# Two more blocks of transposed x by DMA transposes, with the order tables written anew, in a kernel of chunk-selected attention and a gated MLP

## The chip, the cores and the metric

The kernel runs on one core of a Trainium2 chip. The time is device microseconds of one execution (the core's span and what lies around it). Times of a kernel are given as the median of several runs; the trace is of one more execution, which has a time of its own.

## What is computed

For each of 4 batches and 8 heads, 768 queries of 64 elements attend to keys that are taken in chunks of 32. Each query picks six chunks by an upper bound on its scores, and attends causally within them. The heads, side by side, are x; a gated MLP with a mixing over the sequence follows:

```python
k_min = np.min(k_chunks, axis=3)          # k in chunks of 32
k_max = np.max(k_chunks, axis=3)
ub = sum(max(q * k_min, q * k_max))       # one bound per query and chunk
ub = np.where(causal, ub, -1e9)
top_chunks = np.argsort(ub)[..., -6:]
scores = q @ k.T / sqrt(64)               # masked: chosen chunks, causal
x = softmax(scores) @ v                   # heads side by side: 4 x 768 x 512
h = gelu(x @ w_in)                        # tanh form; 512 -> 1024
u, v = h[..., :512], h[..., 512:]
v_n = (v - mean(v)) / sqrt(var(v) + 1e-6) * g_ln
v_s = w_sg @ v_n + b_sg                   # over the 768 positions
out = x + (u * v_s) @ w_out
```

## The kernel before

The work goes by pairs of heads, 16 of them (p, or r where the scores of an earlier pair are meant), four pairs to a batch. A pair has these steps.

- *Loads* (`load_rows`, L541; `load_v`, L552): rows of k, q and v come in as kn, qn and vn, 128 rows to a partition block, all issued by SyncE (SP). Three buffers of each go round.
- *Transposes of k and q* (`kside` L635, `qside` L679, through `rows_T` L559): TensorE (PE) transposes 128×128 blocks in f32 into PSUM (tile PSG, L562). VectorE (DVE) reduces k to a minimum and a maximum for each chunk (W, L657), and ACT or DVE copies k and q out (KA, qT; the copies have the lines of the helper `copier`, L301 on ACT, L302 on DVE and GpSimd (POOL)). POOL or ACT casts qT to QA, and rT is the positive part of qT (L690 or L693). For the last four pairs k is transposed by DMA (L590) instead, and its extremes by DVE.
- *Selection* (`select` L708, `select_full` L761): PE forms the bounds (L730, L777), DVE transposes them (U), finds the eight largest (L747, L797), compares (Dn) and transposes back (Dt, L757, L805). From pair 4 on, rows of Dt are copied into QA by DMA (L810), so that one matmul adds the mask; for the first four pairs PE adds it with IND by matmuls of its own (L893).
- *Scores and softmax* (`scores` L862, `scores_full` L826): PE multiplies into PSC (L887, L847), ACT takes the exponential into E (L902, L853), POOL clears what lies above the diagonal (L909, L858).
- *Values* (`head` L913): PE multiplies E by vx, which holds v and a column of ones (L925, L932); DVE takes the reciprocal of the sum (L940) and writes the scaled rows to XS (L942).
- *Transposed x* (`xtrans` L947): one block of 128 columns of x, that is one pair, is transposed into xT. Either PE does six 128×128 transposes in bf16 into PSUM (L959) and DVE or ACT copies the block out, or one DMA transpose issued by SP does it all (L951). The tuple XDMA (L327) names the blocks (batch, dk) that go by DMA: before, all four of batch 2 and three of batch 3.

When the four blocks of a batch are there, `moe_h` and `moe_g` (L965, L1027) run the MLP: PE multiplies xT by w_in (L974 for the half that is normalized, L1018 for the other); ACT takes the Gelu (L979, L1023), which needs another function table than the exponential; DVE takes means and variances (L987, L989); POOL the root (L1004); DVE the normalization (vhat, L1007). PE mixes over the sequence (L1035), DVE scales, adds the bias and multiplies by u (L1053, L1057), PE multiplies by w_out (L1069), DVE adds x (L1086), and SP stores (L1091). xT, uT, vhat and XS are kept twice, for two batches; in the early part parts of them are staging places for w_in, w_out and w_sg.

The batches overlap: while batch b is in the MLP, the pairs of batch b+1 are in attention. What sets the order is not the order of the code. The code makes a list of operations, each with what it reads and writes (1309 of them). The constant TABLE at the end has, for each engine, the list of operation numbers in the order in which the engine runs them; the PSUM bank of each tile ("slots"); the engine of each operation that may run on several ("choice", one letter each); and a few filler matmuls at the start. `place` and `link` (L101, L123) add the waits that this order needs: an engine runs its list in order, and waits by semaphore for what it reads, for a bank to come free, and for a buffer. All DMAs of the kernel are in SP's list, so one whose data is not there yet holds those behind it.

Of the kernel before, what the change touches and what calls it, by code (L numbers as in the profile page):

```python
# [261 lines left out]
def _build(nc, ctx, q, k, v, w_in, g_ln, w_sg, b_sg, w_out, out):  # L262
# [64 lines left out]
    XDMA = tuple((2, d) for d in range(NDK)) + tuple((3, d) for d in range(3))  # L327
# [213 lines left out]
    def load_rows(p, nm, src, dst):  # L541
        s = p % NQS
        for h0, h1 in ((0, 1), (1, 2)) if p < SPLIT else ((0, 2),):
            for i in range(2):
                j0, j1 = 3 * h0, 3 * h1
                P.op("act" if i == 1 and p < BOTH else "sp", lambda e, i=i, j0=j0, j1=j1: e.dma_start(
                    dst[s][:, j0:j1, i, :], bass.AP(src.tensor, (2 * p + i) * S * DH + 128 * DH * j0,
                                                    [[DH, 128], [128 * DH, j1 - j0], [1, DH]])), dmac(),
                     (nm, p, i, h0), writes=[(nm, s, h, i) for h in range(h0, h1)], dma=f"{nm}{s}_{i}{h0}",
                     xfer=XROW * (h1 - h0) / 2, bulk=NBULK)  # L550
# [8 lines left out]
    def rows_T(src, t, hf):  # L559
        def tr(e):  # L560
            for j in range(3):
                r = e.matmul(t.ap()[:, 128 * j:128 * j + 128],  # L562
                             src[:, 3 * hf + j].rearrange("p i d -> p (i d)"), identF[:], is_transpose=True)
            return r
        return tr
# [69 lines left out]
    def kside(p):  # L635
# [4 lines left out]
        for h0, h1, t in [(hf, hf + 1, ps_g.tile((0, 1, 2, 3))) for hf in range(2)]:  # L640
            ts = [t]

            def tr(e, h0=h0, ts=ts):
                for x, t in enumerate(ts):
                    r = rows_T(kn[s], t, h0 + x)(e)
# [33 lines left out]
    def qside(p):  # L679
        s, w, r = p % NQS, p % NW, p % NR  # L680
        for hf in range(2):
            t = ps_g.tile((0, 1, 2, 3))
            P.op("pe", rows_T(qn[s], t, hf), pe32(*[128] * 3), ("qtr", p, hf), reads=[("qn", s, hf, 0), ("qn", s, hf, 1), "identF"],
# [445 lines left out]
    small_loads()  # L1129
    prep(2)  # L1130
# [9 lines left out]
    for p in range(4, NP + 4):  # L1140
# [4 lines left out]
        if r < NW and HALF < NP:  # L1145
# [31 lines left out]
    "act": (  # L1177
# [9 lines left out]
    "dve": (  # L1187
# [16 lines left out]
    "pool": (  # L1204
# [82 lines left out]
```

## Time and profile before

| what | value |
|---|---|
| median of 3 runs | 208.07 us (207.67 to 208.27) |
| the profiled execution's own time | 208.08 us |
| its span, first to last instruction | 206.0 us |
| PE busy | 197.5 us |
| DVE busy | 186.0 us |
| ACT busy | 162.1 us |
| POOL busy | 92.6 us |
| HBM read and written | 24.87 MB and 6.39 MB |

The span is cut by the first and the last instruction of the program; 2.1 us lie outside it. Busy times are of instructions, and they count an instruction that waits inside its pipeline as busy. PE and the loading of its weights (PEld) overlap. In the rows that follow, "x6" is a count of instructions, a time in us from the start of the span comes first in the timeline and in the chain of waits, and in brackets stands how long the engine was idle before the instruction and what ended that. SPq is the queue of SP. An issue is the instruction that starts a DMA; its data lands later.

### The profile page before, as it was taken

Reading aid. Unit: us, or ns where it says so; the run is one execution under the profiler, and the core shown is the slowest. Engines: PE = TensorE matmul, PEld = TensorE weight load, DVE = VectorE, ACT = ScalarE, POOL = GpSimd, SP = SyncE. Lnnn points to the kernel's source line nnn. Section 1 sums busy time; section 2 is a strip of 40 time slices with the busy share of each in tenths; the row PEclk is TensorE's granted clock in tenths of the full one; section 3 lists DMA queues with packets and bytes.
Section 4 is the critical chain, followed back from the end, with each engine's and each line's share of the span. In section 5 each row is a group of like instructions: output and inputs, shape, how many; then the busy total and the mean of one; then the engine's idle time right before and its main releaser. Section 6 shows DMA issues by size and latency. Waiting matters only on the chain.

```text
span 206.0 us, 5868 instructions
## 1 busy us (share of the span) xinstructions
PE 197.5 (96%) x2294; PEld 131.8 (64%) x2306; DVE 186.0 (90%) x536; ACT 162.1 (79%) x238; POOL 92.6 (45%) x143
## 2 busy tenths in 40 slices
PE   7899999989999999999999999999999999999993
PEld 2547768745775769688456767787456676455551
DVE  4798999989999999999999999998999677897994
ACT  2799999998899988898999889999868986353000
POOL 5254658754665099573534157577221551030000
PEclk9999999999999999999999999999999999999999
DMA  7999999999899769969899947958562445304026
GB/s 150 218 218 219 226 227 307 320 331 234 216 257 235 162 189 234 219 144 189 215 222 221 209 97 194 220 117 86 92 80 41 105 140 112 120 3 151 2 103 253
DMA packets 98378, 36.45 MB, mean 177 GB/s; under 512 B 91952, under 2 KB 93488, under 8 KB 98352
## 3 DMA queue, kind: packets, MB, share of 16 engines
q1 hardware_dynamic: 98352, 36.09, 78.7%
q8 instruction: 18, 0.29, 0.6%
q14 instruction: 8, 0.07, 0.1%
HBM read 24.87 MB, written 6.39 MB: 152 GB/s over the span
## 4 chain that ended last, share of the span: by engine, by line
PE 75%; DVE 10%; ACT 8%; DMA 2%; issue 2%; SPq 1%; DVEq 0%
PE PSG L1035 15%; PE PSC L847 11%; PE PSG L1069 9%; PE PSG L1018 7%; PE PSG L562 7%; PE PSG L925 6%; PE PSG L974 6%; PE PSC L887 3%; ACT E L853 3%; PE PSG L932 2%; PE PSG L777 2%; DMA kn<-in_k_dram 2%; ACT E L902 2%; PE PSC L893 2%; PE PSG L730 2%
## 5 line engine op out<-in xcount | busy, mean ns | idle before, releaser
L853 ACT ACTIVATE E<-PSC 128x1024 bf16<-128x1024 f32 (+1 forms) x72 | 63.2, 915 | 6.7 <-PE PSC L847 5.1
L847 PE MATMUL PSC<-QA,KA 128*128 128x128 bf16 (+2 forms) x336 | 37.7, 246 | 0.2 <-ACT E L853 0.2
L1035 PE MATMUL PSG<-wsgT,vhat 128*128 128x384 bf16 x192 | 34.3, 326 | 0.3 <-DVE vhat L1007 0.3
L858 POOL TENSOR_SCALAR_AFFINE_SELECT E<-E 128x768 bf16<-128x768 bf16 x24 | 20.7, 865 | 24.3 <-ACT E L853 24.3
L847 PEld LDWEIGHTS PSC<-QA,KA 128*128 128x128 bf16 x336 | 24.4, 98 | 8.5 <-ACT E L853 1.5
L657 DVE TENSOR_REDUCE W<-PSG 128x12 f32<-128x384 f32 x48 | 24.2, 546 | 3.2 <-PE PSG L562 3.1
L1035 PEld LDWEIGHTS PSG<-wsgT,vhat 128*128 128x128 bf16 x192 | 18.4, 98 | 11.2 <-DVE vhat L1007 0.5
L1018 PE MATMUL PSG<-xT,winb 128*128 128x384 bf16 x128 | 23.4, 326 | 0.1
L1023 ACT ACTIVATE uT<-PSG 128x384 bf16<-128x384 f32 x32 | 14.5, 492 | 11.2 <-PE PSG L1018 10.8
L1053 DVE SCALAR_TENSOR_TENSOR PSG<-PSG,glnT,bsgbc 128x384 f32<-128x384 f32 x32 | 19.2, 618 | 4.2 <-PE PSG L1035 4.2
L974 PE MATMUL PSG<-winb,xT 128*128 128x512 bf16 x92 | 21.7, 380 | 0.9 <-DVE xT L302 0.6
L1069 PE MATMUL PSG<-woutb,uT 128*128 128x512 bf16 (+1 forms) x92 | 21.6, 370 | 0.4
L302 POOL CAST QA<-qT 64x768 bf16<-64x768 f32 (+1 forms) x19 | 15.6, 821 | 13.9 <-ACT qT L301 13.5
L902 ACT ACTIVATE E<-PSC 128x1024 bf16<-128x1024 f32 (+1 forms) x24 | 20.8, 920 | 0.7 <-PE PSC L893 0.5
L979 ACT ACTIVATE vgb<-PSG 128x512 f32<-128x512 f32 x24 | 14.0, 597 | 7.6 <-PE PSG L974 7.5
L925 PE MATMUL PSG<-vx,E 128*128 128x65 bf16 x480 | 19.4, 194 | 0.1
L925 PEld LDWEIGHTS PSG<-vx,E 128*128 128x128 bf16 x480 | 17.3, 98 | 1.8 <-DVE XS L942 0.3
L942 DVE TENSOR_TENSOR XS<-PSG,rden 128x384 bf16<-128x384 f32 x32 | 17.5, 552 | 0.7
L1018 PEld LDWEIGHTS PSG<-xT,winb 128*128 128x128 bf16 x128 | 12.2, 98 | 8.9 <-ACT uT L1023 0.5
L1057 DVE TENSOR_TENSOR uT<-PSG,uT 128x384 bf16<-128x384 f32 x32 | 17.1, 548 | 0.4
L987 DVE BATCH_NORM_STATS2 stats<-vgb 128x6 f32<-128x512 f32 x24 | 15.9, 683 | 0.8 <-ACT vgb L979 0.7
L974 PEld LDWEIGHTS PSG<-winb,xT 128*128 128x128 bf16 x96 | 8.7, 98 | 11.7 <-ACT vgb L979 2.1
(107 smaller groups left out, 363.9 us busy)
## 6 DMA issues: line engine op xcount, KB each, us to landing
kn<-in_k_dram SPq DMA_DIRECT2D x32, 192.0 KB, 4.4
qn<-in_q_dram SPq DMA_DIRECT2D x32, 192.0 KB, 4.5
vn<-in_v_dram SPq DMA_DIRECT2D x16, 384.0 KB, 4.7
out_dram<-osb SPq DMA_DIRECT2D x18, 256.0 KB, 2.5
uT<-in_moe_w_sg_dram SPq DMA_DIRECT2D x4, 384.0 KB, 5.7
vgb<-in_moe_w_in_dram SPq DMA_DIRECT2D x3, 512.0 KB, 7.8
out_dram<-vgb SPq DMA_DIRECT2D x5, 256.0 KB, 2.1
QA<-Dt SPq DMA_DIRECT2D x24, 36.0 KB, 2.0
```

Source lines behind the costliest of these rows:

```text
L657: P.op("dve", lambda d, m=m, op=op, src=src, h0=h0, h1=h1: d.tensor_reduce(W[w][:, m, 12 * h0:12 * h1].rearrange("p (h c) -> p h c", h=h1 ...
L847: r = e.matmul(t.ap()[:, o:o + n], KA[w][i][:, 128 * kb:128 * kb + 128], QA[w][i][:, q0:q0 + n], start=True, stop=True)
L853: P.op("act", lambda e, t=t, c0=c0, c1=c1, i=i: e.activation(E[es][:, i, c0:c1], t.ap()[:, 0:c1 - c0], ACTF.Exp, scale=SCALE), act(c1 - c0 ...
L858: P.op("pool", lambda g, ev=ev: g.affine_select(ev, ev, pattern=[[0, NT], [1, 128]], compare_op=ALU.is_ge, fill=0.0, base=0, channel_multi ...
L902: P.op("act", lambda e, t=t, c0=c0, c1=c1, n=n: e.activation(E[es][:, :, c0:c1], t.ap().rearrange("p (i x) -> p i x", i=2)[:, :, 0:n], ACT ...
L925: r = e.matmul(t.ap()[:, 65 * qb:65 * qb + 65], E[es][:, i, a:a + 128], vx[w][:, kb, i, :], start=first, stop=False, skip_group_check=True)
L942: P.op("dve", lambda d: d.tensor_tensor(XS[:, b % 2, hh // 2, :, i * DH:(i + 1) * DH], pv3()[:, :, 0:DH], rden[rs][:].rearrange("p (j o) - ...
L974: r = e.matmul(t.ap()[:, 0:F], xT[s][:, dk, 128 * qt:128 * qt + 128], winb[:, dk, F:DFF], start=(dk == 0), stop=(dk == NDK - 1))
L1018: r = e.matmul(t.ap()[:, 0:TG], winb[:, dk, 128 * fb:128 * fb + 128], xT[s][:, dk, TG * tg:TG * tg + TG], start=(dk == 0), stop=(dk == NDK ...
L1035: r = e.matmul(t.ap()[:, 0:TG], vhat[s][:, sb, 128 * fb:128 * fb + 128], wsgT[:, sb, TG * tg:TG * tg + TG], start=(sb == 0), stop=(sb == N ...
L1053: P.op("dve", lambda d, t=t, fb=fb, tg=tg: d.scalar_tensor_tensor(t.ap()[:, 0:TG], t.ap()[:, 0:TG], glnT[:, fb:fb + 1], bsgbc[:, TG * tg:T ...
L1069: r = e.matmul(t.ap()[:, 0:c1 - c0], gT[s][:, fb, 128 * qt:128 * qt + 128], woutb[:, fb, c0:c1], start=(fb == 0), stop=(fb == NF - 1))
```

## The change

Blocks (1, 0) and (1, 1), the first two of the second batch, are put into XDMA. Each loses its six PE transposes and its copy out of PSUM (both copies were DVE's) and becomes one operation of SP. Two PSUM tiles less are taken. The list has 1307 operations, and their numbers after the two blocks move by one and two. In SP's new list the block of pair 5, (1, 1), comes 91st and the block of pair 4, (1, 0), 93rd, with a load of v (pair 10) between them; just ahead of them stand a row of Dt for pair 8 and a load of q (pair 12).

All of TABLE is new: the five orders, the banks and the letters. Besides the two blocks, 58 operations have another engine than before: the lists of DVE, ACT and POOL go from 408, 228 and 139 operations to 404, 225 and 144. At the start ACT's list now begins with two copies of IND (L428), where it began with a copy of CMb (L445); POOL's makes IND's two passes (L424) one right after the other, with one pass of CMb (L440) moved ahead of them; and a cast of QA for pair 1 is on ACT, ahead of its first exponential.

The diff also has a branch that loads rows three to a partition and transposes them so, for the entries of a tuple N3, which is empty; and it moves the call of `mask_rows` for pairs from HALF up to NW to another place, where both of these are 4.

```diff
-    XDMA = tuple((2, d) for d in range(NDK)) + tuple((3, d) for d in range(3))
+    N3 = ()
+    XDMA = tuple((1, d) for d in range(2)) + tuple((2, d) for d in range(NDK)) + tuple((3, d) for d in range(3))
...
     def load_rows(p, nm, src, dst):
         s = p % NQS
+        if (nm, p) in N3:
...
+            return
...
-    def rows_T(src, t, hf):
+    def rows_T(src, t, hf, n3=False):
...
     small_loads()
+    for r in range(HALF, NW):
+        mask_rows(r)
...
-        if r < NW and HALF < NP:
+        if r < HALF and HALF < NP:
             mask_rows(r)
...
 TABLE = {
     "pe": (
-        "1 43 47 52 54 77 81 59 86 88 104 100 186 192 93 190 184 111 109 155 162 194 188 151 160 242 236 116 238 240 198 "
+        "1 43 47 54 52 77 81 59 88 86 100 104 186 192 93 190 184 160 111 109 151 194 188 155 162 242 236 116 202 240 238 "
...
     "sp": (
...
-        "413 347 412 411 553 554 615 298 488 408 409 485 407 551 415 410 350 482 614 612 540 552 613 660 661 663 588 609 "
-        "616 662 608 664 589 611 610 541 506 721 722 697 724 862 555 859 723 649 860 503 861 842 928 509 650 894 863 698 "
+        "413 554 126 552 411 553 346 485 551 488 408 298 407 614 410 482 613 415 409 659 612 611 540 350 661 658 608 660 "
+        "616 615 556 609 722 610 662 607 695 587 859 541 857 720 719 647 721 861 503 588 696 648 840 506 860 509 892 858 "
...
     "filler": (
-        "43:8 54:1 81:2"),
+        "43:8 52:1 81:2"),
```

(In the new list of SP, 616 is block (1, 1), 615 the load of v for pair 10 and 556 block (1, 0).)

More of the change, by code (lines that the diff above doesn't have):

```diff
@@ L542, in load_rows @@
         s = p % NQS
+        if (nm, p) in N3:
+            for h in range(2):
+                P.op("sp", lambda e, h=h: e.dma_start(
+                    dst[s][:].rearrange("p j i d -> p (j i d)")[:, TG * h:TG * h + TG].rearrange("p (i x) -> p i x", i=2),
+                    bass.AP(src.tensor, (2 * p * S + TG * h) * DH, [[3 * DH, 128], [S * DH, 2], [1, 3 * DH]])), dmac(),
+                     (nm, p, h, 3), writes=[(nm, s, h, i) for i in range(2)], dma=f"{nm}{s}_{h}0", xfer=XROW / 2, bulk=NBULK)
+            return
         for h0, h1 in ((0, 1), (1, 2)) if p < SPLIT else ((0, 2),):
@@ L557, in load_v @@
             ("vn", p, 0), writes=[("vn", s)], dma=f"vn{s}", xfer=1880, bulk=NBULK)
-    def rows_T(src, t, hf):
+    def rows_T(src, t, hf, n3=False):
         def tr(e):
             for j in range(3):
+                if n3:
+                    r = e.matmul(t.ap()[:, 0:TG].rearrange("p (x t) -> p t x", t=3)[:, j],
+                                 src[:].rearrange("p j i d -> p (j i d)")[:, TG * hf:TG * hf + TG].rearrange(
+                                     "p (i t d) -> p t i d", i=2, t=3)[:, j], identF[:], is_transpose=True)
+                    continue
                 r = e.matmul(t.ap()[:, 128 * j:128 * j + 128],
@@ L644, in tr @@
                 for x, t in enumerate(ts):
-                    r = rows_T(kn[s], t, h0 + x)(e)
+                    r = rows_T(kn[s], t, h0 + x, ("kn", p) in N3)(e)
                 return r
@@ L682, in qside @@
             t = ps_g.tile((0, 1, 2, 3))
-            P.op("pe", rows_T(qn[s], t, hf), pe32(*[128] * 3), ("qtr", p, hf), reads=[("qn", s, hf, 0), ("qn", s, hf, 1), "identF"],
+            P.op("pe", rows_T(qn[s], t, hf, ("qn", p) in N3), pe32(*[128] * 3), ("qtr", p, hf), reads=[("qn", s, hf, 0), ("qn", s, hf, 1), "identF"],
                  writes=[t], alloc=t)
@@ L1162 @@
     "pe": (
[14 rows of a table removed]
-    "act": (
[9 rows of a table removed]
-    "dve": (
[16 rows of a table removed]
-    "pool": (
[13 rows of a table removed]
[14 rows of a table added]
+    "act": (
[9 rows of a table added]
+    "dve": (
[16 rows of a table added]
+    "pool": (
[14 rows of a table added]
     "slots": (
-        "0132032103013202320333100010001132101220101011331220101110002003230000111233101022200321230101121321323320000311"
-        "1100012112100010122131231201110020033030100110213030322102101203021213233202020013010001111310101121112000010113"
-        "03101011323121013300211302202112100213122010001120010100031100103110011032313330013303100231203011302123"),
+        "3120032313020122323313031310101001202131010113112112000110000301210000111131303023233120231021123123202321030111"
+        "0100132310110001203200231000111220013101100213011201213213110023113212210121013210011033330101100333201011013210"
+        "010100301230210112321013031132122110122101110001010011201100100310011003303230113310020213001323100032"),
     "choice": (
-        "aapdadappapdaadaapppadpddppppdpdpdpdpapadadaapdpappadpdpaadapaappapddpdpdaaapadppapdapapaaaapaapappdapapaaaadaap"
-        "pppddddddddapaappppdadpaapppaddapaappppaaapaappppdddddddppaapaappappppaappppppaappdppaddpdaddpdpddddddddddddd"),
+        "aadadpapappaaapaapapddpaappppdpdpapapaaadapdapppppppdpddadadpadppppddpapaaddpadppppddpapaaaapaappppdapapdaaadadp"
+        "pppdddddddadpaappppaapadpappaapaappppdaapaapappaddddddppaappppppppppaapaapapaapddpdapdppadpdppddddddddddddd"),
     "filler": (
-        "43:8 54:1 81:2"),
+        "43:8 52:1 81:2"),
 }
```

97 rows, old and new, of the table TABLE are left out of this document.

## The prediction

> **What bounds the kernel now.** I read the page first, then the busy time by stage, then the chain of waits, and last the rows around the place of the change. The page:
>
> ```profile
> span 206.0 us, 5868 instructions
> ...
> PE 197.5 (96%) x2294; PEld 131.8 (64%) x2306; DVE 186.0 (90%) x536; ACT 162.1 (79%) x238; POOL 92.6 (45%) x143
> ```
>
> TensorE (PE) is the fullest engine, with VectorE (DVE) close behind. An average over the whole run says little, so here are the stretches around the place of the change, and one late stretch for comparison:
>
> ```profile
> 88.00:92.00 4.00, 4.00 (x77) 3.75 (x74) 4.00 (x10) 3.97 (x6) 3.35 (x4) 1.00 0.57 127
> 92.00:96.00 4.00, 3.89 (x75) 3.42 (x73) 3.90 (x11) 3.44 (x6) 1.98 (x3) 1.00 1.13 237
> 96.00:100.00 4.00, 3.79 (x22) 1.92 (x21) 4.00 (x7) 3.94 (x7) 0.67 (x2) 1.00 0.57 143
> 152.00:156.00 4.00, 4.00 (x42) 2.64 (x41) 4.00 (x28) 3.02 (x8) 0.86 (x1) 1.00 0.51 98
> ```
>
> The columns are the stretch, its length, the busy time of PE, PEld, DVE, ACT and POOL, the granted clock, the share of the DMA engines, and GB/s. From 88 to 92 us PE and DVE are both full and ACT nearly so. No engine is the bound by itself: work taken from one of them alone leaves the others where they are. The clock is granted in full. The chain of waits, in order of time (start, duration, what), shows which engine carries the end of the kernel at the places that matter here:
>
> ```profile
> 12.53 0.85 ACT IND L428
> ...
> 14.06 1.94 ACT E L902 x2
> ...
> 85.39 0.69 DVE osb L1086
> ...
> 88.71 0.47 DVE xT L302
> ...
> 89.87 0.44 DVE xT L302
> ...
> 94.69 0.67 PE PSG L959 x12
> ...
> 97.53 1.28 ACT L979
> 98.83 0.61 ACT vgb L979
> 99.48 2.76 PE PSG L974 x12
> ```
>
> At 12 to 16 us the chain is on ACT. At 85 to 92 us it is on DVE, and the two copies of xT that the change removes (88.71 and 89.87) are pieces of it. At 94.69 it is on PE, in the twelve transposes of the other two blocks. At 97.5 to 99.5 us it is on ACT again: the load of the Gelu table, the first Gelu, and then the matmul that waits for its bank. So the change takes work from two engines that are full and in the chain, and it ends just ahead of a place where a third is.
>
> **The change part by part.** (1) PE loses twelve transposes. What six cost while PE is fed is read from the chain: x12 took 0.67 us at 94.69, and those twelve are the same work for the other two blocks of this batch. So PE loses 0.67 us.
>
> (2) DVE loses the two evacuations, 0.47 + 0.44 = 0.91 us by the chain, or 2 × 542 = 1.08 us by the first row of the group rows below. These sit in the same stage as the PE work. As both engines are full there, the stage shortens by what the less relieved one loses: 0.67 us, and not the sum of both.
>
> (3) SyncE (SP) gets two DMA transposes, and xT waits for their landing. The trace has seven of these already, for the later batches (duration of the issue and then time to landing, min/median/max), and eight of another tile:
>
> ```profile
> L951 SPq DMA_TRANSPOSE xT<-XS x7: 1210/1289/1924, 130.8 to 173.4; - x7
> ...
> DMA to landing us min/median/max: 2.7/2.8/4.3
> ```
>
> ```profile
> L590 SPq DMA_TRANSPOSE KA<-wsb x4: 1225/1296/2398, 127.8 to 164.3; - x4
> ...
> DMA to landing us min/median/max: 2.7/2.9/6.1
> ```
>
> Is that hidden? These are the rows for when the data is there, and for when it is needed:
>
> ```profile
> 87.51 0.54 DVE L942 TENSOR_TENSOR XS<-PSG,rden 128x384 bf16<-128x384 f32 x1
> ...
> 88.63 0.55 DVE L302 COPY xT<-PSG 128x768 bf16<-128x768 bf16 x1
> ...
> 89.10 0.77 DVE L805 STREAM_TRANSPOSE Dt<-Dn 128x576 bf16<-128x576 bf16 x1
> ...
> 89.90 0.55 SPq L810 DMA_DIRECT2D QA<-Dt  x1
> ...
> 90.49 0.58 SPq L554 DMA_DIRECT2D vn<-in_v_dram  x1
> ...
> 91.11 0.71 SPq L546 DMA_DIRECT2D qn<-in_q_dram  x1
> ```
>
> ```profile
> 96.46 2.37 PEld L974 LDWEIGHTS PSG<-winb,xT 128*128 128x128 bf16 x12
> ...
> 99.48 0.55 PEld L974 LDWEIGHTS PSG<-winb,xT 128*128 128x128 bf16 x4 [0.65 <-ACT vgb L979]
> ```
>
> The last block of XS that they need is complete at 87.51 + 0.54 = 88.05. In the new SP order the block of pair 5 goes out behind a row of Dt and a load of q, and the block of pair 4 behind that and a load of v. Dt ends at 89.87 now; in the new DVE order one xT copy (0.55) and the osb addition (0.69) no longer stand ahead of it, so it ends near 88.6. Then 0.55 (row of Dt), 0.71 (q), 1.29 (first transpose) and 0.58 (v) put the second transpose's issue at 91.8. With the median of 2.8 us it lands at 94.6. The first matmul that reads it begins at 96.46 now and 0.67 earlier after the change, at 95.8. The transfer is hidden with 1.2 us to spare, and I cost it at nothing; what hides it is the scores, transposes of q and k and the other two blocks on PE between 91.8 and 95.8. With the longest landings of the rows, 4.3 and 6.1, it would come at 96.1 and 97.9, which is 0.3 and 2.1 us too late. PE already waits 0.65 us at 99.48 for the Gelu, and that much lateness costs nothing. So the bounds of this cost are 0 and 2.1 − 0.65 = 1.45 us; a gain is excluded, since the transfer delivers xT later than PE and DVE did. I take 0, by the row of the same tile. On SP the two issues add 2 × 1.29 = 2.6 us, ahead of the other rows of Dt for pairs 8 and 9 and loads for pairs 11 to 14. Their readers, the scores of pair 9 and the first half of pair 8 and the transposes of later pairs, stand behind the value matmuls of batch 1 in the new PE order, which alone take longer than 2.6 us (2.76 for twelve in the chain, of 24), so nothing queued there is due within the delay.
>
> The Trainium skill, "VectorE: DVE Perf Modes", section "Rules for kernel authors", speaks against this part: it wants a 128×128 transpose on TensorE when PSUM will do, and DMA only otherwise. Its section "The three transpose paths" gives 1309 ns by DMA against 390 ns by TensorE for one such block. By an estimate from that page six blocks one after another are 7.9 us, the landing would be at 99.7, and the sum would rise by 99.7 − 95.8 − 0.65 = 3.2 us. The trace disagrees: whole transposes of six blocks land in 2.7 to 4.3 us there.
>
> (4) All five orders, the banks and the engines of 58 operations are new. Only one part of this can be priced by itself, the start. ACT's first instruction and POOL's mask passes now:
>
> ```profile
> 5.72 0.44 ACT L445 ACTIVATE CMb<-CMb 64x288 bf16<-64x288 bf16 x1 [3.64 <-POOL CMb L440]
> ...
> 8.22 0.84 ACT L301 ACTIVATE QA<-qT 128x768 bf16<-128x768 f32 x1
> ```
>
> ```profile
> 2.99 0.81 POOL L424 TENSOR_SCALAR_AFFINE_SELECT IND<-IND 32x768 bf16<-32x768 bf16 x1 [0.57 <-DVE IND L407]
> ...
> 4.24 0.81 POOL L424 TENSOR_SCALAR_AFFINE_SELECT IND<-IND 32x768 bf16<-32x768 bf16 x1
> ```
>
> ACT sits idle until 5.72, for a mask that POOL makes late. In the new order it begins with copies of IND. Those need POOL's two passes, between which nothing stands any more, so they end at 2.99 + 2 × 0.81 = 4.6, or 4.7 with one instruction moved ahead of them. ACT starts 1.0 us earlier. It also gets one more cast of QA ahead of its first exponential, 0.84 us. As the chain at 12 to 16 us is on ACT, that is worth −0.2 us. The bounds are +0.84 (if PE's first transposes hold ACT up, so that the early start is lost) and −1.0.
>
> The remaining moves shift work from DVE to POOL and ACT. The larger ones are one copy of winb, two each of rT and wsgT that leave DVE, net of two each of KA and qT that come to it:
>
> ```profile
> L302 DVE COPY xT<-PSG 128x768 bf16<-128x768 bf16 x8 | 4.3, 542 | 0.1
> L302 DVE CAST KA<-PSG 128x384 bf16<-128x384 f32 (+1 forms) x7 | 3.8, 539 | 0.0
> L302 DVE COPY qT<-PSG 128x384 f32<-128x384 f32 x5 | 2.7, 545 | 0.5 <-PE PSG L562 0.4
> L302 DVE COPY wsgT<-PSG 128x768 bf16<-128x768 bf16 x4 | 2.2, 550 | 0.1
> L693 DVE TENSOR_SCALAR rT<-qT 128x576 f32<-128x576 f32 x2 | 1.8, 910 | 0.0
> L302 DVE CAST winb<-xT 128x1024 bf16<-128x1024 f32 x1 | 0.7, 683 | 0.0
> ```
>
> With the two xT copies DVE loses 2 × 542 + 2 × 910 + 2 × 550 + 683 − 2 × 539 − 2 × 545 = 2.5 us. PE loses only 0.67 us, and it was busy in 4.00 of 4 us both at 88 and at 152, so I take nothing for the rest; the bounds are 0 and 2.5 − 0.67 = 1.8 us of gain. The new branch for three-row loads stands behind an empty list, and the two mask loops do what they did, since both of their limits are 4: that part of the diff costs nothing.
>
> The sum: the profiled execution took 208.08 us, of which the span is 206.0. Less 0.67 and 0.2 gives 207.2 us. The median of the runs shown, 208.07, is the same to a hundredth, so it needs no shift.
>
> **The rivals.** *Late landing (slower).* The second transpose goes out at 91.8, into the stretch 92 to 96 in which the DMA share is 1.13, the highest of the four. Rows of Dt show what that does: in the issues from 84 to 100 us against those of the whole run (median us to landing last),
>
> ```profile
> QA<-Dt SPq DMA_DIRECT2D x4, 36.0 KB, 4.3
> ```
>
> ```profile
> QA<-Dt SPq DMA_DIRECT2D x24, 36.0 KB, 2.0
> ```
>
> That is 2.3 us more. The two transposes add load of their own: at 152 to 156, with two of them in flight, 0.51 × 4 = 2.0 us of all the engines. So landing may take 2.8 + 2.3 + 2.0 = 7.1 us, until 98.9; PE would be held 98.9 − 95.8 = 3.1 us at the first value matmul of batch 1, of which 0.65 is covered. The time is 207.2 + 2.45 = 209.7. It decides the sign from a landing of 6.1 us on, where the loss of 1.45 gives 208.7. Against it: the seven transposes of the same tile took at most 4.3, and the one of 6.1 among the others is the only evidence of such a time. The page's rule above is this rival with another price. I give it 0.18.
>
> *ACT takes the gain (no change).* The chain at 97.5 to 99.5 is on ACT, and the new ACT order has one more evacuation of KA (about 0.5 us) ahead of the table load, taken from DVE. If that wait ends last, the 0.67 us of PE become a longer wait for the Gelu, and 0.5 of them are lost: 208.08 − 0.67 + 0.5 = 207.9. For it speaks the wait of 0.65 us at 99.48; against it, ACT loses work overall. Chance 0.29.
>
> *DVE was the bound (more gain).* If PE's full rows hide waits within its pipeline, all of DVE's relief counts: 208.08 − 2.5 = 205.6; half of the 1.8 on top of 207.2 is 206.3. For it speaks the chain on DVE at 85 to 92; against it, PE's 4.00 of 4. Chance 0.12.
>
> **How the numbers follow.** The forecast of 207.2 has 0.41; its own spread, by the start's bounds, is 206.4 to 208.0. About 0.3% is what a measurement of this kernel can tell from no change, so faster means under 207.45 and slower above 208.7. Faster: 0.35 of the forecast, all 0.12 of the last rival and 0.04 of the second, 0.51. Within: 0.06 of the forecast, 0.25 of the second, 0.01 of the first, 0.32. Slower: 0.17 of the first. The range runs from 206.3, half of DVE's relief, to 208.9, a landing a little beyond 6.1 us; that leaves out about 0.05 below and 0.1 above.
>
> **What would show it.** Right: no xT copies near 88 to 90 on DVE; two L951-type transposes issued between 88 and 93, landing within 3 to 4 us; the first value matmul of batch 1 (L974) up to 1 us earlier and waiting for an evacuation or a bank, not for a DMA; ACT's first work near 4.7 us. Wrong: PE waiting for a DMA that writes xT; the first exponential later than 14.06; the lead at 96 us given back before the last output.

## The result, and the profile after

The changed kernel is slower: median 210.69 us (210.19 to 212.08, four runs) against 208.17 us for the kernel before on the same chip, a ratio of 1.0118 with a 95% interval of 1.0087 to 1.0148. The forecast was 207.2, and its range ended at 208.9. The profiled execution took 210.19 us. Executions that took over 1.5% longer than the fastest of their kernel are left out of the times below.

From here on the lines of the code are those of the changed kernel, 13 further down than before in this part (the value matmul L974 is now L987, the DMA transpose L951 now L964). The page of the changed kernel begins so:

```profile
span 208.4 us, 5850 instructions
...
PE 195.4 (94%) x2280; PEld 131.3 (63%) x2294; DVE 184.4 (88%) x532; ACT 160.5 (77%) x235; POOL 94.7 (45%) x148
```

PE's busy time fell by 2.1 us and DVE's by 1.6, and the span grew by 2.4. So PE waits more, and the stretches say where (same columns as before: the stretch, its length, PE, PEld, DVE, ACT, POOL, the granted clock, the share of the DMA engines, GB/s):

```profile
88.00:92.00 4.00, 4.00 (x77) 3.73 (x75) 3.97 (x10) 4.00 (x6) 3.24 (x4) 1.00 0.37 79
92.00:96.00 4.00, 4.00 (x77) 3.66 (x75) 3.82 (x11) 3.60 (x7) 2.51 (x3) 1.00 1.14 208
96.00:100.00 4.00, 1.10 (x8) 0.62 (x8) 3.70 (x6) 2.69 (x4) 2.67 (x5) 1.00 0.57 120
```

Up to 96 us nothing is wrong. From 96 to 100 PE works 1.10 us where it worked 3.79 before: 2.7 us are gone in one stretch. The timeline of PE shows the instruction, and the view of the transposes (issues, who waited, time to landing) shows what it waited for:

```profile
99.27 4.91 PE L987 MATMUL PSG<-winb,xT 128*128 128x512 bf16 x22 [2.90 <-DMA xT<-XS]
```

```profile
L964 SPq DMA_TRANSPOSE xT<-XS x9: 1211/1287/2185, 91.0 to 174.3; - x9
...
who waited for it (us, times):
  PE PSG L987: 2.9, 1
...
DMA to landing us min/median/max: 2.8/3.1/5.8
```

Of nine transposes one made PE wait, once, 2.90 us. It is the longest of the nine, 5.8 us, and the chain of waits says which:

```profile
88.69 0.70 DVE Dt L818
89.41 0.53 SPq L823
89.98 1.02 SPq L554
91.04 1.32 SPq L964
92.41 0.57 SPq L562
93.03 5.78 DMA xT<-XS
98.81 0.46 issue
99.27 5.13 PE PSG L987 x23
```

Here the chain is no longer on DVE, PE and ACT but on SP and the DMA: Dt, its row, the load of q, the first transpose (block (1, 1)), the load of v, and then the second transpose (block (1, 0)), issued at 93.03 and landed at 98.81.

That this wait is the loss shows when the same operations on PE are set side by side (start after minus start before): +0.57 us at 65.7, −0.15 at 91.7 (a score of pair 7), −0.05 at 95.4 (a score of pair 8), then +2.56 at the first value matmul of batch 1, +2.16 at the bounds of pair 10, and +2.28 for the last output.

### The profile page after: what moved, and what is told of

It reads as the page before. It is cut to its first block, busy times and chain, and to the rows that moved or that the text cites. A ratio compares the mean times of both kernels' runs of the same rounds, so it can differ in the third digit from the quotient of the medians.

```text
span 208.4 us, 5850 instructions
## 1 busy us (share of the span) xinstructions
PE 195.4 (94%) x2280; PEld 131.3 (63%) x2294; DVE 184.4 (88%) x532; ACT 160.5 (77%) x235; POOL 94.7 (45%) x148
## 4 chain that ended last, share of the span: by engine, by line
PE 74%; DMA 9%; DVE 8%; SPq 3%; ACT 3%; issue 1%; DVEq 0%
PE PSG L1048 15%; PE PSC L860 11%; PE PSG L1082 9%; PE PSG L1031 8%; PE PSG L987 7%; PE PSG L575 7%; DMA kn<-in_k_dram 7%; PE PSG L938 5%; DMA xT<-XS 3%; PE PSC L900 3%; PE PSG L743 2%; PE PSG L790 2%; SPq L554 2%; PE PSG L945 2%; PE PSC L906 2%; DVE U L799 1%
## 5 line engine op out<-in xcount | busy, mean ns | idle before, releaser
L987 PE MATMUL PSG<-winb,xT 128*128 128x512 bf16 x92 | 21.8, 379 | 3.1 <-DMA xT<-XS 2.9
L1017 POOL TENSOR_TENSOR rstd<-rstd,neghalf 128x3 f32<-128x3 f32 x8 | 7.3, 909 | 24.3 <-DVE rstd L1014 24.1
L703 POOL TENSOR_SCALAR rT<-qT 128x576 f32<-128x576 f32 x16 | 10.6, 665 | 15.1 <-ACT qT L301 13.2
```

The lines of the kernel that those rows point to most:

```text
L987: r = e.matmul(t.ap()[:, 0:F], xT[s][:, dk, 128 * qt:128 * qt + 128], winb[:, dk, F:DFF], start=(dk == 0), stop=(dk == NDK - 1))
```

## The experiments

The theory: the second transpose lands late because it is issued late and behind the bulk load of v (384 KB), and the wait is the loss. The rivals: the new orders lose the time anyhow; or ACT stands behind PE and keeps what is won; or SP, which has 2.6 us more to do, owes the time to others later. Most of the edits move entries in SP's list alone. In the diffs 658 and 660 are the loads of k and q of pair 12, 608 and 609 are rows of Dt of pairs 8 and 9, 616 is block (1, 1), 615 and 662 are the loads of v of pairs 10 and 11, and 556 is block (1, 0). "New" kernels have the changed kernel's orders; "old" ones have the lists of before with the two blocks taken out of PE and DVE and put into SP's list (in the changed kernel's numbering). All compute the whole of the reference.

**Block (1, 0) early, new orders.**

```diff
-658 608 660 616 615 556 609
+658 556 608 616 660 615 609
```

> The changed kernel with one move in SP's list: block (1, 0) goes out ahead of the row of Dt for pair 8, where SP stands idle from 86.8 to 89.4 us, and block (1, 1) right behind that row, ahead of the loads of q and v. Late landing: both blocks land before 94 us, PE waits for no DMA at the first value matmul, and the time falls by the wait of 2.9 us less the 0.65 us that PE waits there for the Gelu anyway, from 210.7 to about 208.4, level with the kernel before (208.2) within 0.5 us. Rival, the new orders are what costs: the place of the DMA wait is taken by waits for ACT or DVE, and the time stays above 209.7.

Measured: 209.04 us (12 runs) against 208.60 for before, ratio 1.0022 (0.9995 to 1.0048). Block (1, 0) lands at 91.11, block (1, 1) at 93.27, and no value matmul waits for a DMA. But the chain of this kernel has another wait:

```profile
93.32 0.46 PE PSG L938 x15
93.97 1.02 issue
94.99 0.84 PE PSG L575 x6
```

PE stands 1.02 us ahead of the transposes of q for pair 12. ("Issue" says that the profile shows no releaser; the load of q, pushed behind the transposes, now goes out at 92.08 instead of 89.98 and lands 2.8 us later, at 94.9, and PE goes on at 94.99.) So most of the loss was the late block, and the early block took a part of it from q.

**Both blocks ahead of the loads of q and v, new orders.**

```diff
-658 608 660 616 615 556 609
+658 608 616 556 660 615 609
```

> The changed kernel with the loads of q (pair 12) and v (pair 10) moved from ahead of block (1, 0) to behind it: Dt row, (1, 1), (1, 0), q, v. The two transposes follow each other directly. If it is the queue of loads that holds the second one: it is issued near 91.3, lands in 3.0 to 3.5 us at 94.6, and the time is 208.4 as with the early issue. Rival, two transposes one right after the other hold each other up: the second still takes near 5.8 us, lands at 97.1, and PE waits about 1 us; 209.0 or more.

Measured: 211.56 us, 1.0154 (1.0115 to 1.0192). Block (1, 0), right behind the other transpose, lands 2.83 us after its issue, where it took 5.78 behind the load of v. Still the kernel is the slower one. SP's timeline, the chain and two stretches show why:

```profile
89.14 3.30 SPq L964 DMA_TRANSPOSE xT<-XS  x2
92.48 0.59 SPq L554 DMA_DIRECT2D qn<-in_q_dram  x1
```

```profile
92.95 2.55 issue
95.50 1.14 PE PSG L575 x6
```

```profile
94.00:96.00 2.00, 0.51 (x4) 0.54 (x5) 0.00 (x0) 0.00 (x0) 0.11 (x1) 0.98 1.15 258
96.00:98.00 2.00, 2.00 (x17) 1.81 (x16) 1.02 (x2) 1.02 (x3) 0.51 (x1) 0.50 1.15 220
```

The two transposes hold SP for 3.3 us, and the load of q goes out at 92.48 and lands 2.9 us later, at 95.40. PE stands 2.55 us, until 95.50; from 94 until then DVE and ACT stand too. Behind it the granted clock is 0.50, until 99.31 (the last section has the rows), so that PE is "busy" and does half as much. The wait and the clock together took the kernel from 0.99 us ahead of before to 2.71 behind.

**Old orders, block (1, 0) early.** The list of before with `556` ahead of the loads and `616` in the middle, so that the change is made alone:

```diff
+556 658 659 661 587 616 608 615 660 607
```

> The orders, banks and engines of the kernel before, with only the two blocks put to DMA: their PE transposes and copies are taken out of the lists, (1, 0) is issued ahead of the loads of k for pair 12 and (1, 1) right behind the copy of KA for pair 9. By the prediction's own first term PE and DVE lose 0.67 us and no DMA is waited for: 208.2 - 0.7 = 207.5. Rival, ACT takes the gain: PE is at the Gelu earlier and waits longer, 207.9 to 208.2.

Measured: 209.78 us (eight runs), 1.0074 (1.0046 to 1.0102). Landings at 88.55 and 93.39, in time. It is q again, as the chain of this kernel says (PE stands 0.93 us for it, and 0.47 before that for a row of Dt):

```profile
92.65 4.37 DMA qn<-in_q_dram
97.06 0.87 PE PSG L575 x6
```

**Old orders, the changed kernel's places.**

```diff
+658 659 661 587 608 660 616 615 556 607
```

> The same old orders with the two blocks at the places that the changed kernel gives them on SP: Dt row of pair 8, load of q (pair 12), block (1, 1), load of v (pair 10), block (1, 0). Late landing: the second block lands near 98.8, PE waits 2 to 3 us at the first value matmul, and the time is 2 us above the run with the early issue, near 209.7. Rival, the new orders are what costs: no more than 0.5 us above it.

Measured: 211.51 us (four runs, one of them 208.73, the others 211.42 to 211.82), 1.0117 (1.0061 to 1.0174), about the loss of the changed kernel. Block (1, 0) is issued at 93.95, behind the load of v, and lands at 99.64, 5.69 later; the first value matmul of batch 1 starts 3.24 us later than before. Late landing costs this with either set of orders.

**q and block (1, 0) both early, new orders.**

```diff
-658 608 660 616 615 556 609
+658 660 556 608 616 615 609
```

> The changed kernel; in SP's list the load of q for pair 12 and block (1, 0) now both go out ahead of the row of Dt for pair 8, where SP stands idle, block (1, 1) right behind that row, then the load of v. The runs so far moved the wait from block (1, 0) to the load of q that the transposes were put ahead of. If SP's order at this place is all that costs: PE waits for neither, the wait of 1.0 us at 94 us in the first early run is gone, and the time is 0.2 to 1.0 us under that run, between 0.5 us under the kernel before and level with it. Rival, any place on SP that is given to the transposes makes something else late: a new wait of PE for a DMA of 0.5 us or more appears, and the time stays level with the first early run.

Measured: 208.62 us against 208.49 for before, 0.9999 (0.9976 to 1.0023). Landings at 93.14 and 93.84; the wait for q of the first two kernels is gone and so is the loss. But nothing is won either, and the rival is right too: a new wait stands in the timeline of PE, ahead of a score of pair 8.

```profile
93.50 0.60 PE L860 MATMUL PSC<-QA,KA 128*128 128x128 bf16 x7 [1.18 <-ACT KA L301]
```

The row names a copy of KA on ACT that ended at 93.38. But the row of Dt for pair 8, which this matmul reads through QA, landed at 93.41, 4.02 us after its issue behind block (1, 0). In the next kernel but one, which has the same lists for PE and ACT, the same matmul starts at 92.40, before that copy of KA (93.13), and the row of Dt had landed at 91.92. So it is the row of Dt that PE waits for.

**The same, old orders.**

```diff
+658 659 661 660 556 608 616 615 587 607
```

> The same with the orders, banks and engines of the kernel before: load of q (pair 12), block (1, 0), row of Dt, block (1, 1), load of v, and only then the copy of KA for pair 9. Without a DMA wait the prediction's first term is all that is left, 0.67 us under the kernel before. Rival, ACT takes the gain: within 0.3 us of the kernel before. Rival of the run before this one: a wait for a DMA again, 0.5 us or more above the kernel before.

Measured: 212.05 us (five runs), 1.0178 (1.0118 to 1.0237). There is no loss at the first value matmul (0.15 us ahead of before until 120.9), but SP is late with what follows (from 97 to 122 us by 3.2 us or more, mostly 3.2 to 3.6), and a row of Dt for pair 10 goes out at 120.87 instead of 117.66. The groups of waits show who pays:

```profile
PE PSC L860 <- DMA QA<-Dt: 1.6, 2, 1.3
```

(The columns are the time waited in all, how often, and the longest.) PE is 2.06 us late at 127. The rival "SP owes the time later" is right for the old orders: their list for SP has no room for two more issues.

**The load of v behind block (1, 0), new orders: one entry moved.**

```diff
-658 608 660 616 615 556 609
+658 608 660 616 556 615 609
```

> The changed kernel with one load moved: v of pair 10 from ahead of block (1, 0) to behind it. The load of q stays where it was. If a load that is issued just ahead is what makes the landing long: issued at 92.4, landing in 3 to 3.5 us at 95.6, no wait, 2.2 us under the changed kernel. Rival, the two loads already out (q, and those of the stage) are enough: it lands after 5 us at 97.5, PE waits about 1.2 us, and the time is 1.2 us under the changed kernel.

Measured: 208.03 us (206.78 to 208.83, ten runs) against 208.49, a ratio of 0.9952 (0.9916 to 0.9989). This beats both kernels, the one before by half a microsecond only. SP's timeline, the stretch and the chain:

```profile
89.87 1.38 SPq L554 DMA_DIRECT2D qn<-in_q_dram  x1
91.29 2.64 SPq L964 DMA_TRANSPOSE xT<-XS  x2
93.98 0.58 SPq L562 DMA_DIRECT2D vn<-in_v_dram  x1
```

```profile
96.00:100.00 4.00, 3.65 (x19) 1.51 (x18) 4.00 (x7) 3.98 (x7) 0.80 (x2) 1.00 0.84 193
```

```profile
97.31 1.28 ACT L992
98.60 0.61 ACT vgb L992
99.25 2.76 PE PSG L987 x12
```

The two issues take 2.64 us together where they took 1.32 and 2.19 with the load of v between them, the second block lands 2.82 us after its issue, at 95.48, and PE works 3.65 of 4 us from 96 to 100. One load of 384 KB, moved by one place, is 2.66 us by the medians (210.69 less 208.03), and 3.0 by the distances from the kernel before, which was measured beside each of the two. The chain also shows where the gain ends: at ACT's table load and Gelu. PE's first value matmul starts 0.33 us earlier than before, the matmul behind the Gelu 0.23 (99.25 against 99.48).

**Both blocks on PE and DVE again, new orders.** XDMA as before; the four operations go back into the new lists, at places and banks chosen by hand:

```diff
-    XDMA = tuple((1, d) for d in range(2)) + tuple((2, d) for d in range(NDK)) + tuple((3, d) for d in range(3))
+    XDMA = tuple((2, d) for d in range(NDK)) + tuple((3, d) for d in range(3))
```

> The new orders and engines with both blocks back on PE and DVE, put into the lists where their data is ready, in banks 0 and 2. It tells the new orders from the DMA transposes. If the DMA transposes alone cost: level with the kernel before within 0.5 us, and about 0.7 us above the run with q and x early, the price of the twelve transposes. Rival, the new orders are worse by themselves: 1 us or more above the kernel before.

Measured: 210.09 us, 1.0069 (1.0034 to 1.0103), 2.06 us above the kernel with one entry moved. Its chain (lines numbered as before) runs through the copies that the change had removed:

```profile
88.05 0.35 PE PSG L959 x6
88.42 0.56 DVE xT L302
...
93.48 0.48 DVE xT L302
```

So the DMA transposes are worth up to 2.06 us when they land in time, and the new orders without them lose up to 1.6 (210.09 less 208.49). Both are upper bounds, since better places for the four operations may exist.

**The load of v behind, old orders.**

```diff
+658 659 661 587 608 660 616 556 615 607
```

> The orders, banks and engines of the kernel before, with SP's list at this place as in the faster run: row of Dt, load of q, block (1, 1), block (1, 0), and only then the load of v. If only the landing counts: the second block is issued near 93.9, lands in 2.8 us at 96.7, PE waits at most 0.3 us, and the time is 0.4 to 0.7 us under the kernel before. Rival, SP's time is owed later: the two issues set everything behind them on SP back by 2.6 us, the old list has no slack until the rows of Dt for pair 10 (due at 122 us), PE waits 1 to 2 us there, and the time is 0.7 to 1.7 us above the kernel before.

Measured: 210.75 us, 1.0100 (1.0067 to 1.0133). The landing is as good as with the new orders, 2.82 us, at 95.49. The chain then follows the load of v, which goes out 3.5 us later than before:

```profile
94.00 0.59 SPq L562
94.63 0.73 SPq L823
95.40 6.71 DMA vn<-in_v_dram
102.24 0.84 POOL vx L302
103.08 0.40 POOL W L689 x2
103.47 0.64 POOL rT L703
104.25 1.27 PE PSG L790 x32
```

The next load (pair 11) lands at 102.1; POOL copies it and only then makes rT, and the bounds of pair 10 wait on PE, 1.40 us later than before. The debt falls due there, and not at the rows of Dt that the rival named; 1.22 us more are lost before a score at 132.84. The new orders let SP fall behind at this place without such a wait.

**Two loads of v ahead of block (1, 0), new orders, one run.** If the load ahead sets the landing, twice the load should double the delay.

```diff
-658 608 660 616 615 556 609
+658 608 660 616 615 662 556 609
```

> The changed kernel with a second load of v (pair 11) put between the first and block (1, 0): the suspected cause doubled. If a transpose lands only after the loads that were issued ahead of it (2.2 us after the load of v in the changed kernel): issued near 93.7, the second load of v lands near 100, the block near 102, and PE waits about 6 us in place of 2.9; the time is 3 us above the changed kernel, near 213.5. Rival, the long landing has to do with the place and not with the load: 5.8 us from its issue as before, 99.4, 0.6 us above the changed kernel.

Measured: 212.33 us. The wait and the stretch behind it:

```profile
PE PSG L987 <- DMA xT<-XS: 3.9, 1, 3.9
```

```profile
100.00:104.00 4.00, 4.00 (x14) 1.49 (x13) 0.27 (x1) 0.90 (x2) 0.00 (x0) 0.65 0.70 168
```

The block went out at 93.15 and landed at 99.40, 6.24 later and not near 9. The theory's sizes fall: the second load was down at 98.70, not near 100, and the block 0.7 us behind it, not 2.2. The rival named 99.4 for the landing, and that is what came, but its reason fails: at the same place, with the loads behind it, the block took 2.82 us.

What holds is the order. In all thirteen traces every DMA of SP's list (179 or 181 in each) lands later than the one issued before it, without an exception, and the block is in none of them there before a load that was issued ahead of it. Issue and landing, in us:

| DMA | changed kernel | v behind |
|---|---|---|
| row of Dt, pair 8 | 89.41, 91.66 | 89.30, 91.92 |
| q, pair 12 | 89.98, 93.41 | 89.87, 93.53 |
| block (1, 1) | 91.04, 94.35 | 91.29, 94.38 |
| block (1, 0) | 93.03, 98.81 | 92.66, 95.48 |
| v, pair 10 | 92.41, 96.58 | 93.98, 99.05 |
| row of Dt, pair 9 | 95.26, 99.02 | 94.61, 99.25 |

In the changed kernel v goes out ahead of block (1, 0), in the other behind it. The row that follows lands at about the same time in both; only who comes first has changed. In the seven kernels in which a bulk load goes out right ahead of block (1, 0), the block lands 0.6 to 2.4 us after that load has landed: v 96.58 and block 98.81 in the changed kernel, 97.28 and 99.64 in the old orders' late one, 98.70 and 99.40 here. Why these 0.6 us become 2.4 in some was not tried apart.

**One entry moved, and a load of w_in early as well.** At 42.6 us of the changed kernel ACT waits 0.95 us for a load of w_in, which the new list issues at 33.65 instead of 28.99. Here that load (75) goes forward, on top of the moved load of v:

```diff
-172 131 173 121
+172 131 75 173 121
-68 70 75 295 294
+68 70 295 294
```

> The faster run (load of v behind block (1, 0)) with one more move on SP: the last load of w_in goes out some 4 us earlier, ahead of the loads of k and q for pair 5. In the new orders ACT waits 0.8 us for it at 42 us and the first value matmul of batch 0 is 0.45 us late. If that wait ends last there, the first value matmul comes 0.4 us earlier and the time falls by 0.3 to 0.5 us under the faster run. Rival: PE then waits for the loads of pair 5 that were pushed back, and nothing is gained.

Measured: 209.00 us (ten runs), 1.0010 (0.9984 to 1.0036). At the bounds of pair 4 PE is 1.04 us behind before, where it was 0.25 without this edit: PE stands 0.82 us at 35.30, until a load of k that now goes out behind w_in is down (35.21). And ACT's wait was not the one that counted, as the next section shows.

## Why the prediction was wrong

**The step that failed** is in part (3): "The transfer is hidden with 1.2 us to spare, and I cost it at nothing". It took 2.8 us, the median landing of the same tile, "by the row of the same tile". Those seven were issued at 130 us and later; this one was put behind a 384 KB load into the busiest stretch for DMA of the four shown, and took 5.78. The tile was the wrong likeness. The right one stood in the text of the first rival: the rows of Dt from the same stretch, 4.3 against 2.0 us, the only rows there that showed what this place does to a landing. And the order was in the trace: a load of v issued at 93.17 landed at 99.55, and the five DMAs issued after it, rows of 36 KB among them, landed from 99.77 on. When the load is moved behind it, the same block in the same stretch does land in 2.82, and the forecast's mechanism holds.

**The issue time** was a second miss in that step: 91.8 forecast, 93.03 measured. Dt ended at 89.39 instead of 88.6, and q's issue took 1.02 instead of 0.71. The first of these is in part a matter of the execution: PE was 0.55 us late at 82.6 here, and in the six traces whose lists are the same up to that point it was between 0.28 ahead and 0.74 behind; where it was 0.28 ahead, Dt's row went out at 88.57. With 2.8 us of landing these 1.2 us would just have been covered: 95.8, against 96.4 when PE got there.

**The first rival, late landing,** is what happened. It gave a landing at 98.9 (measured 98.81), PE held 3.1 us (2.90) and 209.7 us, and had a chance of 0.18. The landing time agreed in its sum only, by luck: it took 91.8 + 7.1, and it was 93.03 + 5.78. Its reason, a stretch in which all landings are long, is not the one either: in that stretch the block took 2.82 us with the load of v behind it.

**The 0.65 us that it took as covered** were read from the row of the weight loads (PEld). PE itself stood a shorter time there:

```profile
99.48 2.76 PE L974 MATMUL PSG<-winb,xT 128*128 128x512 bf16 x12 [0.15 <-ACT vgb L979]
```

In the changed kernel 0.40 us were made up by that matmul (2.56 behind before it, 2.16 from it on).

**Part (1), PE's 0.67 us,** shows: between 82.6 and 91.7 us, where the two blocks were transposed, PE goes from 0.55 behind to 0.15 ahead, 0.70 in all, and in all seven traces with the two blocks by DMA and the new orders it is 0.70 or 0.71. But in the four with the old orders, where nothing else moves, it is 0.28 each time. So the size agrees, and that it is the transposes alone is not shown. **Part (2)** took nothing for DVE beyond PE's 0.67. The kernel with both blocks back on PE and DVE, 2.06 us slower than the one with v behind, suggests more, but as an upper bound; this stays open.

**Part (3), SP's 2.6 us for nothing,** held with the new orders at the changed kernel's places: it and the kernel with v behind have no new wait for the rows of Dt or for v. It fails with the old ones, where it came due at 104 and 121 us.

**Part (4), the start:** ACT begins at 4.91 us (forecast 4.7, before 5.72), but the first exponential at 13.97 instead of 14.06: 0.09 us and not 0.2. Over all traces it lies between 13.63 and 14.32 with the new orders and between 13.88 and 14.23 with the old, so the gain at the start is not shown.

By 65.7 us PE was 0.57 behind. It had stood for a load of k, which was down at 44.22, after those of w_in:

```profile
44.27 0.55 PE L575 MATMUL PSG<-identF,kn 128*128 128x128 f32 x3 [1.19 <-DMA kn<-in_k_dram]
```

ACT, which had waited for w_in until 42.6, was then waiting for PE. But that PE is late here is not shown to be a price of the new orders. In the traces whose lists are the new or the old ones up to 84 us (six and four), PE lies between 0.42 us ahead of the one trace of the kernel before and 0.86 behind it at 82 us, and both kinds are on both sides. In this one the lead of 0.67 us that was to meet the value matmul at 95.8 was 0.09 (PE got there at 96.37, before at 96.46).

**The other moves,** taken at nothing, do have a price at another place. In the new order of DVE a comparison (Dn) stands ahead of the last normalization of batch 2, and PE, which mixes with it, stands longer. The first row is of the kernel before, the second of the one with v behind:

```profile
156.91 0.82 PE L1035 MATMUL PSG<-wsgT,vhat 128*128 128x384 bf16 x4 [0.26 <-DVE vhat L1007]
```

```profile
157.39 0.97 PE L1048 MATMUL PSG<-wsgT,vhat 128*128 128x384 bf16 x5 [0.90 <-DVE vhat L1020]
```

With the new orders this wait is 0.84 to 0.92 us in all eight traces, with the old ones 0.26 to 0.39 in all five.

**ACT takes the gain** is right in part, once the wait is away: in the kernel with v behind the chain is on ACT until the Gelu lets PE go on at 99.25, and of a lead of 0.33 us 0.23 are left. At 157 us PE goes from 0.25 ahead to 0.46 behind, and its profiled run ends level with before.

**The rule of the Trainium skill,** "VectorE: DVE Perf Modes", "Rules for kernel authors", pointed the right way for the order as it was changed, and the estimate from "The three transpose paths" (207.2 + 3.2 = 210.4 us) came close to the time measured. Its mechanism is not the one here: by that estimate a block would always take 7.9 us, and the same block took 2.82 with the load of v behind it.

## What to carry to other kernels

The time to landing of a DMA belongs to its place in the queue, and not to its kind: find when the transfer issued right ahead of it will be down, above all a bulk load, and count from there. When a queue gets new issues, list each entry that they push back and who reads it; here nearly every place for the transposes moved the wait to another reader (q, a row of Dt, v), and only one order came out ahead of the kernel before, by half a microsecond. And do not count on a lead that is smaller than what two executions of the same lists differ by: here the lead was 0.67 us, and PE came to 82 us up to 0.86 late.

## What the runs showed of the hardware

DMAs on SP's queue land in the order of their issue: all 179 or 181 of them, in all thirteen traces. Block (1, 0) lands 2.82 to 2.84 us after its issue when the entry ahead of it is another transpose (four kernels), 4.0 to 5.3 us when it is a load of k or q (192 KB, four kernels), and 5.7 to 6.2 when it is one or two loads of v (384 KB, three kernels). The size of the load ahead does not tell it alone: block (1, 1), right behind a load of q in six kernels, took 2.9 to 3.3 us. That load of q was itself down 2.9 to 3.7 us after its issue, and the loads right ahead of block (1, 0) took 3.9 to 6.3.

The issue of block (1, 0) holds SP 1.3 us behind a transpose, and 1.5 to 2.8 right behind a load; that of block (1, 1) right behind a load of q took 1.3. So a load ahead does not always lengthen it, and what does stays open.

For the granted clock of PE the place of an idle counts, and not only its length. In the kernel with both blocks ahead of q and v the record of the clock changes at 7.16, 95.90 and 99.31 us; the later two are 26 and 27 times 3.41 us after the first. In the kernel with two loads ahead the changes are at 7.21, 99.37 and 102.79, and those are 27 and 28 times. So stretches of 3.41 us can be laid out in every trace from its first change on. These are the one in which the first of the two kernels stood, and the one behind it; then the one of the changed kernel with most of its idle, and the one behind that:

```profile
92.48:95.90 3.42, 0.87 (x20) 0.78 (x17) 1.23 (x3) 1.33 (x2) 1.57 (x2) 1.00 0.99 214
95.90:99.31 3.41, 3.41 (x25) 2.88 (x23) 1.84 (x4) 2.06 (x4) 0.84 (x1) 0.50 1.13 218
```

```profile
97.26:100.67 3.41, 1.40 (x7) 0.81 (x9) 2.44 (x4) 1.43 (x2) 2.13 (x5) 1.00 0.68 154
100.67:104.08 3.41, 3.41 (x18) 1.38 (x15) 2.47 (x6) 2.96 (x6) 0.00 (x0) 1.00 1.05 208
```

An idle of 2.55 us that lay in one stretch was followed by one stretch at 0.50. So was a whole stretch without work in the kernel with two loads ahead (95.96 to 99.37), whose clock of 0.65 above is that stretch at 0.50 and a rest at 1.00. The 2.90 us of the changed kernel are cut by a border, 2.01 of them lie in one stretch, and the clock stays at 1.00. Over all traces 2.01 us is the longest idle within one stretch that no fall followed. Two other runs of the changed kernel, its two longest, have a mean clock of 0.992, which is what one stretch at 0.50 would give (half of 3.41 us is 0.8% of 209): an estimate, since there is no trace of them.
